# One scale for the a and b weights of a unit, with joint operations over both, and the last four pairs in the raw-query buffer: block-sparse attention followed by a bilinear FFN

## The chip, the cores and the metric

One core of one Trainium2 chip. The metric is the device time of one execution in microseconds (us); lower is better. The profile is one execution recorded by the hardware profiler, and all rows below are from it.

## The reference, cut to what matters

```python
# attention: batch 4, 8 heads, 768 positions, head size 64, blocks of 32
scores = q @ k.T / sqrt(64)
mask = (neighbour blocks) | (first and last block) | (3 sampled blocks per query block)
attn = softmax(where(mask, scores, -1e9))
attn_out = attn @ v
# FFN over the 3072 tokens, model size 512, inner size 1536
x = attn_out.transpose(0, 2, 1, 3).reshape(3072, 512)
out = ((x @ w_a) * (x @ w_b)) @ w_out
```

The inputs reach the kernel as 64-bit words of which it uses parts: the weights have to be put together from two 32-bit halves before they are numbers.

## The kernel before, in words

Every matrix product is made in fp16 with each operand split into a high part and a low part (hi and lo), after a scaling by a power of two that keeps them in range. TensorE multiplies hi by hi, hi by lo and lo by hi.

The attention runs in 96 units, one for a batch and a block of 32 queries. 88 of them are sparse (eight blocks of keys), eight are dense (the first and the last block of each batch). Eight units make a chunk of 256 tokens; there are 12 chunks, three for a batch. The FFN of a chunk can begin when the outputs of its eight units lie in xT, which is the event x_ready. The FFN runs over 12 inner blocks f of 128 columns. For each (chunk, f) there are 24 matmuls into ab (line 1265), then ScalarE and VectorE form a*b and split it (1282, 1285, 1294, 1297), and 6 matmuls add to the output (1325 to 1327). The first two chunks run f by f in three groups (0 to 5, 6 to 8, 9 to 11), so that they can begin before all the weights are ready.

The order of every engine's instructions is written out ahead by a planner (class Plan): each flow is a generator that yields an operation with an estimated duration or an event, and the planner always takes the operation that can begin first by its own estimates. The engines then execute their lists strictly in order. A changed estimate or a changed flow can thus alter the lists of all engines from that point on.

The weights are the flows weights(n) and weight_parts(n, ...), with n = 3f + i: i = 0 is w_a of block f, 1 is w_b, 2 is w_out. For each there are a load (752) into a raw ring of six slots, three VectorE operations that put the words together (768, 772, 775), a Square on ScalarE that sums into a bound (801), a scale for the three matrices of the block (weight_scale: a GpSimd reduction and four small VectorE operations, 826 to 837), a Copy to the high part on ScalarE (806) and a VectorE operation for the low part (809).

For f = 0 to 7 a and b are put together by joint operations over 1024 columns, into the place in wab that the weights of f + 4 will take later. From the Square on, a and b go separately, with 512 columns each. For f = 8 to 11 there is no such place: a and b are put together separately, in slots of the ring st, which has three slots and also serves w_out and the rows of the output. The three matrices of one block therefore fill that ring.

The buffer rq has one slot. queries(cc) takes it for the raw queries of a chunk and lets it go when the low part of the queries is made (708). The ring's takers are served in the order in which their flows ask for it.

All loads of raw keys and values of batches 1 to 3 wait for the event w_freed, which fires when the last weight has been put together (the raw weights lie in their buffers). The load of q is issued on ScalarE's queue (691), as are those of the weights and of raw keys (491).

Of the kernel before, what the change touches and what calls it, by code (L numbers as in the profile page):

```python
# [11 lines left out]
F32 = mybir.dt.float32  # L12
# [3 lines left out]
AF = mybir.ActivationFunctionType  # L16
# [21 lines left out]
AHEAD = 4  # L38
# [22 lines left out]
R_W, R_W_STEP = 16, 0.2  # L61
# [165 lines left out]
def dve(ns, fn):  # L227
    return [Way("DVE", ns, fn)]


def act(ns, fn):
    return [Way("ACT", ns, fn)]


def pool(ns, fn):
    return [Way("POOL", ns, fn)]


def load_way(moved, fn):

    return [Way("LOAD", 475, fn, moved)]
# [7 lines left out]
def kernel(  # L249
# [13 lines left out]
    nc = tc.nc  # L263
    B, NCH, D, H, CH = q.shape
    NF, P, DM = w_a.shape
# [5 lines left out]
    KT = DM // P  # L271
# [11 lines left out]
    work = ctx.enter_context(tc.tile_pool(name="work", bufs=2))  # L283
# [4 lines left out]
    plan = Plan()  # L288
    rings = {}

    def take(tag, bufs):
        return rings.setdefault(tag, Ring(bufs)).take()
# [5 lines left out]
    wab = wpool.tile([P, NF, 2, 2, KT, P], F16, name="wab")  # L298
# [15 lines left out]


    at_k, at_v, at_q, at_w = 0, B * NG, B * NG + B, B * NG + B + NC
    at_x = at_w + 3 * NF
    n_at = at_x + NC
    bound = const.tile([P, n_at], F32, name="bound")
    bound_v = const.tile([P, B * NG], F32, name="bound_v")  # L320
# [1 line left out]
    scale = const.tile([P, n_at], F32, name="scale")  # L322
    rscale = const.tile([P, n_at], F32, name="rscale")
# [45 lines left out]
    s_sent = {u: Event() for u in units}  # L369
    av_done = {u: Event() for u in units}  # L370
    x_ready = [Event(PER) for _ in range(NC)]
    w_bound = [Event(3) for _ in range(NF)]
    w_known = [Event(hi - lo) for lo, hi in GROUPS]
    all_known = Event(len(GROUPS))
    w_scale = [Event() for _ in range(NF)]
    w_staged = {}
    w_freed = Event(3 * NF)
    w_ready = [Event(3) for _ in range(NF)]
    w_small = [Event() for _ in range(NF)]
    ffn_done = [Event() for _ in range(NC)]  # L380

# [356 lines left out]
    def raw_weights(n, count):  # L738
        half, at = divmod(n % W_BUFS, W_BUFS // 2)
        raw = (  # L740
            stage.rearrange("p g x -> p (g x)"), keysT[1].rearrange("p h s -> p (h s)")
        )[half].bitcast(I32)
        return raw[:, at * 2 * DM : (at + count) * 2 * DM]

    def weights(n):

        f, i = divmod(n, 3)
        both = i == 0 and f + AHEAD < NF
        freed = []
        for m in range(n, n + 1 + both):  # L750
            freed.append((yield from take("w", W_BUFS)))
            yield load_way(1350, lambda m=m: nc.scalar.dma_start(
                raw_weights(m, 1), (w_a, w_b, w_out)[m % 3][f].bitcast(I32)
            ))
        if n + 1 + both < 3 * NF:
            plan.start(weights(n + 1 + both), R_W + R_W_STEP * (n + 1 + both))
        if both:

            if f + AHEAD >= NF // 2:
                yield parked  # L760
            w = wab[:, f + AHEAD].rearrange("p i a c x -> p (i a c x)").bitcast(F32)
            gone = w_staged[f + AHEAD, 0] = w_staged[f + AHEAD, 1] = Event(2)
        else:
            gone = yield from take("st", ST_BUFS)
            w = work.tile([P, DM], F32, tag="st", name=f"w{n}", bufs=ST_BUFS)
        words = raw_weights(n, 1 + both).rearrange("p (x w) -> p x w", w=2)
        o = w.bitcast(I32)
        yield dve(700 if both else 425, lambda: nc.vector.tensor_scalar(
            o, words[:, :, 1], 3, 0x3FFFFFFF, ALU.logical_shift_left, ALU.bitwise_and
        ))  # L770
        ns = 1220 if both else 685
        yield dve(ns, lambda: nc.vector.scalar_tensor_tensor(
            o, words[:, :, 0], 29, o, ALU.logical_shift_right, ALU.bitwise_or
        ))
        end = yield dve(ns, lambda: nc.vector.scalar_tensor_tensor(
            o, words[:, :, 1], -0x40000000, o, ALU.bitwise_and, ALU.bitwise_or
        ))
        for ev in freed:
            ev.fire(end)
            w_freed.fire(end)  # L780
        for m in range(1 + both):
            plan.start(
                weight_parts(n + m, w[:, m * DM : (m + 1) * DM], gone),
                R_W + R_W_STEP * (n + m), end,
            )

    def weight_parts(n, w, gone):
        f, i = divmod(n, 3)
        if i < 2:
            hi, lo = wab[:, f, i, 0], wab[:, f, i, 1]  # L790
            w = w.rearrange("p (c f) -> p c f", c=KT)
            if f >= NF // 2:
                yield parked
            if f >= AHEAD:
                yield w_staged[f, i]
        else:
            hi, lo = woh[:, f, :], wol[:, f, :]
            plan.start(weight_scale(f), R_W + R_W_STEP * n)
        at = at_w + 3 * f + i
        s = scale[:, at : at + 1]  # L800
        end = yield act(800, lambda: nc.scalar.activation(
            hi, w, AF.Square, accum_out=bound[:, at : at + 1]
        ))
        w_bound[f].fire(end)
        yield w_scale[f]
        end = yield act(720, lambda: nc.scalar.activation(hi, w, AF.Copy, scale=s))
        if i == 2:
            plan.start(small_weights(f, hi), R_W + R_W_STEP * n, end)
        end = yield dve(755, lambda: nc.vector.scalar_tensor_tensor(
            lo, w, s, hi, ALU.mult, ALU.subtract  # L810
        ))
        gone.fire(end)
        w_ready[f].fire(end)

    def small_weights(f, hi):
        end = yield act(620, lambda: nc.scalar.activation(
            wos[:, f, :], hi, AF.Copy, scale=1 / G_LOW
        ))
        w_small[f].fire(end)

    def weight_scale(f):

        yield w_bound[f]
        a = slice(at_w + 3 * f, at_w + 3 * f + 3)
        bits = power[:, a].bitcast(I32)
        yield pool(480, lambda: nc.gpsimd.partition_all_reduce(
            power[:, a], bound[:, a], P, bass_isa.ReduceOp.absmax
        ))
        yield dve(150, lambda: nc.vector.tensor_scalar(
            bits, bits, 1, 0x7F800000, ALU.logical_shift_right, ALU.bitwise_and  # L830
        ))
        yield dve(150, lambda: nc.vector.tensor_scalar(
            rscale[:, a], power[:, a], float(2.0 ** 53), float(2.0 ** -80), ALU.mult, ALU.max
        ))
        end = yield dve(160, lambda: nc.vector.reciprocal(scale[:, a], rscale[:, a]))
        w_scale[f].fire(end)
        end = yield dve(212, lambda: nc.vector.scalar_tensor_tensor(
            w3[:, f : f + 1], rscale[:, a.start : a.start + 1],
            rscale[:, a.start + 1 : a.start + 2], rscale[:, a.stop - 1 : a.stop],
            ALU.mult, ALU.mult,  # L840
        ))
        g = group_of(f)
        w_known[g].fire(end)
        if w_known[g].count == 0:
            lo, hi = GROUPS[g]
            end = yield dve(150, lambda: nc.vector.reduce_max(
                w3_max[:, g : g + 1], w3[:, lo:hi], axis=mybir.AxisListType.X
            ))
            group_known[g].fire(end)
            all_known.fire(end)  # L850
            if all_known.count == 0:
                n = len(GROUPS)
                end = yield dve(150, lambda: nc.vector.reduce_max(
                    w3_max[:, n : n + 1], w3_max[:, :n], axis=mybir.AxisListType.X
                ))
                group_known[n].fire(end)

    def group_of(f):
        return next(g for g, (lo, hi) in enumerate(GROUPS) if lo <= f < hi)
# [510 lines left out]
    with tc.manual_schedule():  # L1370
        nc.vector.memset(warm, 0.0)
        nc.vector.memset(bound, 0.0)
        nc.scalar.activation(warm, warm, AF.Exp)
        plan.start(keys(0, 0), -LEAD_K)
        plan.start(load_eye(), -LEAD_K)
        plan.start(queries(0), 0.5 - LEAD_K)
        plan.start(make_tables(), 0)
        plan.start(values(0, 0), -LEAD_V)
        plan.start(weights(0), R_W)
        plan.start(gather_keys(0), -LEAD_G)  # L1380
        plan.start(gather_values(0), -LEAD_G)
        plan.start(attend(*units[0]), 0)
        for cc in range(NC):
            plan.start(norms(cc), R_NOW)
        plan.start(first_products(), R_P1)
        plan.run()
# [69 lines left out]
```

## Time and profile before

| | us |
|---|---|
| median of 3 runs | 872.83 (871.74 to 878.28) |
| the profiled execution | 871.27 |
| span from its first to its last instruction | 869.5 |

So 1.8 us of the profiled execution lie outside its span, and the median stands 1.56 us above it. Busy times in the rows are those of one engine in a stretch; PE is TensorE, DVE is VectorE, ACT is ScalarE, POOL is GpSimd, and a q behind a name is that engine's queue of commands. A line Lnn is a line of the kernel before.

### The profile page before, as it was taken

How to read it: one execution, taken by the hardware profiler on the slowest of the kernel's cores; microseconds unless marked ns; L12 is line 12 of the kernel's file. 1: busy time of each engine (PE TensorE's matmuls, PEld its weight loads, DVE VectorE, ACT ScalarE, POOL GpSimd, SP SyncE). 2: the span in 40 equal slices, each digit the busy share in tenths (PEclk: the TensorE clock that was granted, in tenths of full speed). 3: DMA queues.
4: the chain of work that ended last, by engine and by line, in shares of the span. 5: the costliest groups of instructions: out<-in, count | busy, mean ns of one | idle time of the engine just before them, and what ended most of it. 6: DMA issues, size and time to landing. Idle time of an engine off the chain costs nothing.

```text
span 869.5 us, 24163 instructions
## 1 busy us (share of the span) xinstructions
PE 759.1 (87%) x9136; PEld 561.9 (65%) x9136; DVE 590.8 (68%) x1609; ACT 501.3 (58%) x1191; POOL 191.7 (22%) x428
## 2 busy tenths in 40 slices
PE   2246367599999979999999999999999999999998
PEld 1134245377767757766776667677777677777775
DVE  4979988999788666766576696766677776432222
ACT  6579787866766464774355586644656554332222
POOL 0743253200034232330032242200342310000000
PEclk9996689999999999999999999999999999999999
DMA  8766798795967479896586899767966766610000
GB/s 244 211 182 201 223 228 188 179 246 128 243 172 183 118 155 215 194 176 178 134 166 170 162 209 239 160 152 172 168 143 161 144 138 159 142 44 1 25 2 25
DMA packets 195151, 138.74 MB, mean 160 GB/s; under 512 B 138073, under 2 KB 162650, under 8 KB 195034
## 3 DMA queue, kind: packets, MB, share of 16 engines
q1 hardware_dynamic: 183104, 99.40, 52.3%
q10 hardware_dynamic: 11930, 37.79, 14.4%
q8 instruction: 72, 1.18, 0.6%
q14 instruction: 45, 0.37, 0.1%
HBM read 86.28 MB, written 12.58 MB: 114 GB/s over the span
## 4 chain that ended last, share of the span: by engine, by line
PE 47%; DVE 18%; DMA 18%; ACT 10%; issue 4%; SPq 2%; ACTq 1%; POOL 0%; POOLq 0%; DVEq 0%
PE ab L1265 25%; DMA pt<-hl 6%; PE av L967 5%; PE o L1325 5%; DMA q<-in_q_dram 5%; PE o L1327 4%; PE o L1326 4%; PE s L923 3%; DVE hl L948 2%; DMA VG<-vd 2%; DMA stage<-in_k_dram 2%; DVE QT L708 2%; DVE xT L1236 2%; ACT sm L1049 1%; ACT QT L706 1%
## 5 line engine op out<-in xcount | busy, mean ns | idle before, releaser
L1265 PE MATMUL ab<-xT,wab 128*128 128x256 f16 x3456 | 401.4, 273 | 6.0 <-DVE xT L1236 3.2
L1265 PEld LDWEIGHTS <-wab 128*128 128x128 f16 x3456 | 334.4, 98 | 68.5 <-issue 13.8
L1285 DVE SCALAR_TENSOR_TENSOR a<-a,to_g,ab 128x256 f32<-128x256 f32 x144 | 68.6, 477 | 104.8 <-ACT a L1282 103.7
L1282 ACT ACTIVATE a<-ab,w 128x256 f32<-128x256 f32 x144 | 67.3, 467 | 112.0 <-PE ab L1265 109.6
L1049 ACT ACTIVATE sm<-s,low,cq 128x256 f32<-128x256 f32 x176 | 97.7, 557 | 50.0 <-DVE low L1042 28.2
L948 DVE SCALAR_TENSOR_TENSOR hl<-sm,den,hl 128x256 f16<-128x256 f32 (+1 forms) x208 | 104.8, 512 | 27.7 <-ACT hl L941 25.5
L627 POOL COPY KG<-keysT 128x384 int32<-128x384 int32 x88 | 58.7, 667 | 283.5 <-PE s L923 251.4
L967 PEld LDWEIGHTS <-VG 128*128 128x128 f16 x2688 | 97.9, 100 | 29.3 <-issue 14.7
L1325 PE MATMUL o<-woh,gh 128*128 128x512 f16 x288 | 109.8, 381 | 7.9 <-ACT gh L1294 7.9
L967 PE MATMUL av<-pt,VG 128*128 128x64 f16 x2688 | 104.3, 196 | 11.0 <-DMA VG<-vd 7.4
L1327 PE MATMUL o<-wos,gl 128*128 128x512 f16 x288 | 109.3, 380 | 3.1 <-DVE gl L1297 2.6
L632 POOL COPY KG<-keysT 128x128 int32 x264 | 103.5, 428 | 36.7 <-POOL KG L627 26.3
L1326 PE MATMUL o<-wol,gh 128*128 128x512 f16 x288 | 109.2, 379 | 0.0
L1294 ACT ACTIVATE gh<-a 128x256 f16<-128x256 f32 x144 | 59.4, 413 | 60.6 <-DVE a L1285 55.8
L1297 DVE SCALAR_TENSOR_TENSOR gl<-gh,a 128x256 f16<-128x256 f16 x144 | 63.2, 440 | 34.2 <-ACT gh L1294 33.4
L941 ACT ACTIVATE hl<-sm,den 128x256 f16<-128x256 f32 (+1 forms) x91 | 46.0, 517 | 38.6 <-DMA pt<-hl 27.8
L923 PE MATMUL s<-KG,QT 128*32 128x256 f16 x1408 | 60.1, 295 | 6.6 <-POOL KG L632 6.1
L1236 DVE SCALAR_TENSOR_TENSOR xT<-av,xT 64x256 f16<-64x256 f32 x96 | 40.3, 420 | 33.0 <-ACT xT L1233 31.6
L1039 DVE TENSOR_REDUCE low<-s 128x2 f32<-128x512 f32 x88 | 60.0, 682 | 1.7 <-PE s L923 1.1
L1024 PE MATMUL s<-mrows,ident 128*32 128x192 bf16 (+1 forms) x352 | 25.9, 284 | 37.2 <-ACT sm L1049 25.3
L944 DVE TENSOR_SCALAR hl<-sm,den 128x256 f16<-128x256 f32 (+1 forms) x117 | 42.5, 365 | 19.7 <-DMA pt<-hl 19.4
L1327 PEld LDWEIGHTS <-gl 128*128 128x128 f16 x288 | 28.1, 98 | 42.4 <-DVE gl L1297 10.6
(115 smaller groups left out, 776.9 us busy)
## 6 DMA issues: line engine op xcount, KB each, us to landing
VG<-vd SPq DMA_DIRECT2D x284, 64.0 KB, 2.0
VG<-vd SPq DMA_DIRECT2D x88, 192.0 KB, 3.0
VG<-vd SPq DMA_DIRECT2D x32, 384.0 KB, 3.5
q<-in_q_dram ACTq DMA_DIRECT2D x24, 256.0 KB, 5.7
QT<-QT SPq DMA_DIRECT2D x24, 256.0 KB, 3.8
vd<-vs SPq DMA_DIRECT2D x16, 384.0 KB, 3.3
out_dram<-ou SPq DMA_DIRECT2D x24, 256.0 KB, 2.4
stage<-in_k_dram ACTq DMA_DIRECT2D x12, 384.0 KB, 5.5
```

Of the source, the lines that this page charges most:

```text
L632: nc.gpsimd.tensor_copy(to[:, :, (5 + r) * w : (6 + r) * w], of[:, :, bass.ds(at, w)])
L923: mm(to[h * BLK : (h + 1) * BLK], q_block(cc, i, 4 * hq + h, a), rhs(4 * hq + h), start=(first and a == 0), stop=(a == 1), skip_group_chec ...
L948: t = yield dve(221 + n * 1.03, lambda: nc.vector.scalar_tensor_tensor(lo, sm, over, hi, ALU.mult, ALU.subtract))
L967: mm(av[:, g, i % 2, :], w, pt[:, y, cols], start=(i % 2 == 0 and g == 0 and first and n + m == 0), stop=(last and n == len(terms) - 1 and ...
L1049: t = yield act(750, lambda hq=hq: nc.scalar.activation(sm[:, hq], ps[:, hq], AF.Exp, bias=low[:, at, hq, 0:1], scale=cq[:, cc, hq : hq + ...
L1265: mm(ab[:, i, :], wab[:, f, i, part, kt, :], xc[:, kt, a, :], start=(i == 0 and kt == 0 and part + a == 0), stop=(kt == KT - 1 and a == 1) ...
L1282: yield act(470, lambda: nc.scalar.activation(a_sb, ab[:, 0, :], AF.Copy, scale=w3[:, f : f + 1]))
L1285: t = yield dve(420, lambda: nc.vector.scalar_tensor_tensor(a_sb, a_sb, to_g[:, n : n + 1], ab[:, 1, :], ALU.mult, ALU.mult))
L1297: t = yield dve(460, lambda: nc.vector.scalar_tensor_tensor(gl, gh, -G_LOW, a_sb, ALU.mult, ALU.add))
L1325: mm(po, gh[:, js], woh[:, f, :], start=(f == lo), stop=False)
L1326: mm(po, gh[:, js], wol[:, f, :], start=False, stop=False)
L1327: mm(po, gl[:, js], wos[:, f, :], start=False, stop=(f == hi - 1))
```

## The change

The a and b weights of a block get one scale between them, from one bound over both; w_out keeps its own. The Square, the Copy to the high part and the low part are then made for both in one instruction over 2 x 512 columns, where there were two instructions over 512. The last four blocks also put a and b together by joint operations; their buffer is the one slot of rq in place of two slots of st. The planner's durations are altered to match. The product of the scales in weight_scale uses the shared scale twice.

```diff
-        both = i == 0 and f + AHEAD < NF
+        both = i == 0
...
-        if both:
+        if both and f + AHEAD >= NF:
+            gone = yield from take("rq", 1)
+            w = work.tile([P, H, CH], F32, tag="rq", name=f"w{n}", bufs=1)
+            w = w.rearrange("p h s -> p (h s)")[:, : 2 * DM]
+        elif both:
...
-            gone = w_staged[f + AHEAD, 0] = w_staged[f + AHEAD, 1] = Event(2)
+            gone = w_staged[f + AHEAD] = Event()
...
-        for m in range(1 + both):
-            plan.start(
-                weight_parts(n + m, w[:, m * DM : (m + 1) * DM], gone),
-                R_W + R_W_STEP * (n + m), end,
-            )
+        plan.start(weight_parts(n, w, gone), R_W + R_W_STEP * n, end)
...
-        if i < 2:
-            hi, lo = wab[:, f, i, 0], wab[:, f, i, 1]
-            w = w.rearrange("p (c f) -> p c f", c=KT)
+        if i == 0:
+            hi, lo = (
+                wab[:, f, :, a].rearrange("p i c f -> p i (c f)") for a in range(2)
+            )
+            w = w.rearrange("p (i x) -> p i x", i=2)
...
-        end = yield act(800, lambda: nc.scalar.activation(
+        end = yield act(1240 if i == 0 else 800, lambda: nc.scalar.activation(
             hi, w, AF.Square, accum_out=bound[:, at : at + 1]
         ))
...
-        end = yield act(720, lambda: nc.scalar.activation(hi, w, AF.Copy, scale=s))
+        end = yield act(1140 if i == 0 else 720, lambda: nc.scalar.activation(
+            hi, w, AF.Copy, scale=s
+        ))
...
-        end = yield dve(755, lambda: nc.vector.scalar_tensor_tensor(
+        end = yield dve(1290 if i == 0 else 755, lambda: nc.vector.scalar_tensor_tensor(
             lo, w, s, hi, ALU.mult, ALU.subtract
         ))
...
-        a = slice(at_w + 3 * f, at_w + 3 * f + 3)
+        a = slice(at_w + 2 * f, at_w + 2 * f + 2)
...
             w3[:, f : f + 1], rscale[:, a.start : a.start + 1],
-            rscale[:, a.start + 1 : a.start + 2], rscale[:, a.stop - 1 : a.stop],
+            rscale[:, a.start : a.start + 1], rscale[:, a.start + 1 : a.stop],
```

## Rows read from the trace of the kernel before

**Rows 1.** The page's first part: busy time, share of the span, instructions.

```profile
PE 759.1 (87%) x9136; PEld 561.9 (65%) x9136; DVE 590.8 (68%) x1609; ACT 501.3 (58%) x1191; POOL 191.7 (22%) x428
```

**Rows 2.** Stretches: length, busy PE, PEld, DVE, ACT, POOL (count), granted clock, DMA share, GB/s.

```profile
20.00:60.00 40.00, 10.87 (x134) 7.13 (x134) 33.95 (x79) 24.50 (x53) 21.90 (x34) 1.00 0.74 215
60.00:115.00 55.00, 30.08 (x482) 21.55 (x483) 52.75 (x128) 47.21 (x111) 21.43 (x36) 0.70 0.75 208
115.00:173.00 58.00, 39.49 (x548) 28.40 (x546) 51.15 (x143) 45.69 (x110) 19.74 (x37) 0.96 0.85 195
173.00:252.00 79.00, 78.53 (x830) 59.45 (x830) 68.12 (x185) 52.84 (x124) 7.31 (x21) 1.00 0.82 197
...
296.00:330.00 34.00, 29.59 (x418) 21.46 (x417) 24.53 (x71) 19.88 (x51) 9.19 (x22) 1.00 0.62 136
```

**Rows 3.** PE's timeline, first products of chunks 1 and 3: start, us, [idle before, releaser].

```profile
171.75 0.38 PE L1265 MATMUL ab<-xT,wab 128*128 128x256 f16 x2 [0.85 <-ACT xT L1233]
173.14 2.56 PE L1265 MATMUL ab<-xT,wab 128*128 128x256 f16 x22 [1.01 <-DVE xT L1236]
...
326.06 2.56 PE L1265 MATMUL ab<-xT,wab 128*128 128x256 f16 x22 [0.67 <-DVE xT L1236]
```

**Rows 4.** Groups by line and form, whole span: busy us, mean ns of one.

```profile
L708 DVE SCALAR_TENSOR_TENSOR QT<-q,scale,QT 64x2048 f16<-64x2048 f32 x12 | 28.2, 2347 | 5.8 <-ACT QT L706 5.7
L706 ACT ACTIVATE QT<-q,scale 64x2048 f16<-64x2048 f32 x12 | 24.0, 2000 | 2.4 <-DVE scale L399 2.2
L809 DVE SCALAR_TENSOR_TENSOR wab<-wab,scale 128x512 f16<-128x512 f32 x16 | 12.1, 760 | 0.0
L806 ACT ACTIVATE wab<-wab,scale 128x512 f16<-128x512 f32 x16 | 10.8, 711 | 0.5 <-DVE scale L835 0.4
L801 ACT ACTIVATE wab<-wab 128x512 f16<-128x512 f32 x16 | 9.9, 622 | 6.2 <-DVE wab L775 5.9 <-DVE den L1054 0.2
L772 DVE SCALAR_TENSOR_TENSOR w<-stage,w 128x512 int32<-128x512 int32 x10 | 6.8, 676 | 0.0
L809 DVE SCALAR_TENSOR_TENSOR wab<-w,scale,wab 128x512 f16<-128x512 f32 x8 | 5.8, 747 | 0.4 <-ACT wab L806 0.4
L772 DVE SCALAR_TENSOR_TENSOR wab<-stage,wab 128x1024 int32<-128x1024 int32 x4 | 4.9, 1237 | 0.0
L801 ACT ACTIVATION_READ_ACCUMULATOR wab<-wab 128x1 f32 x16 | 3.0, 189 | 0.0
```

**Rows 5.** Waits from 20 to 173 us: waiter, awaited, us in total, times, longest.

```profile
DVE hl L948 <- ACT hl L941: 10.5, 4, 4.6
...
PE s L1024 <- ACT sm L1049: 22.7, 9, 4.6
```

**Rows 6.** DVE's timeline: words of f = 8 to 11, and the queries of chunk 3.

```profile
146.72 0.76 DVE L768 TENSOR_SCALAR w<-stage 128x512 int32<-128x512 int32 x2
162.95 0.42 DVE L768 TENSOR_SCALAR w<-stage 128x512 int32<-128x512 int32 x1
169.90 2.34 DVE L708 SCALAR_TENSOR_TENSOR QT<-q,scale,QT 64x2048 f16<-64x2048 f32 x1 [0.47 <-ACT QT L706]
176.50 0.41 DVE L768 TENSOR_SCALAR w<-keysT 128x512 int32<-128x512 int32 x1
192.40 0.42 DVE L768 TENSOR_SCALAR w<-stage 128x512 int32<-128x512 int32 x1
...
214.39 0.69 DVE L775 SCALAR_TENSOR_TENSOR w<-keysT,w 128x512 int32<-128x512 int32 x1
```

**Rows 7.** ScalarE's timeline: loads of block 8's b, chunk 3's queries, batch 1's first keys.

```profile
136.30 0.33 ACTq L752 DMA_DIRECT2D stage<-in_moe_w_b_dram  x1
...
157.50 0.61 ACTq L691 DMA_DIRECT2D q<-in_q_dram  x1
...
215.12 0.96 ACTq L491 DMA_DIRECT2D stage<-in_k_dram  x2
```

**Rows 8.** PE's timeline: the first scores of batch 1 (unit 24).

```profile
237.06 0.83 PE L923 MATMUL s<-keysT,QT 128*32 128x384 f16 x16
```

More of the change, by code (lines that the diff above doesn't have):

```diff
@@ L316 @@
     at_k, at_v, at_q, at_w = 0, B * NG, B * NG + B, B * NG + B + NC
-    at_x = at_w + 3 * NF
+    at_x = at_w + 2 * NF
     n_at = at_x + NC
@@ L371 @@
     x_ready = [Event(PER) for _ in range(NC)]
-    w_bound = [Event(3) for _ in range(NF)]
+    w_bound = [Event(2) for _ in range(NF)]
     w_known = [Event(hi - lo) for lo, hi in GROUPS]
@@ L377 @@
     w_freed = Event(3 * NF)
-    w_ready = [Event(3) for _ in range(NF)]
+    w_ready = [Event(2) for _ in range(NF)]
     w_small = [Event() for _ in range(NF)]
@@ L794, in weight_parts @@
             if f >= AHEAD:
-                yield w_staged[f, i]
+                yield w_staged[f]
         else:
@@ L798, in weight_parts @@
             plan.start(weight_scale(f), R_W + R_W_STEP * n)
-        at = at_w + 3 * f + i
+        at = at_w + 2 * f + (i > 0)
         s = scale[:, at : at + 1]
-        end = yield act(800, lambda: nc.scalar.activation(
+        end = yield act(1240 if i == 0 else 800, lambda: nc.scalar.activation(
             hi, w, AF.Square, accum_out=bound[:, at : at + 1]
```

## The prediction

> **What bounds the kernel now.** I read the page's first part, then busy time by stretch, then the timeline of TensorE where the stretches change, then the waits of the early stretch.
>
> The first part [rows 1] names TensorE, with 87% of the span. That is an average over two different halves, and the table of stretches [rows 2] separates them. From 173 to 252 us TensorE is busy 78.53 of 79 us. From there on it nearly always has an FFN product to do, and what is taken from VectorE or ScalarE buys nothing. Before 173 us it is busy less than 70% of the time, with part of that at a granted clock of 0.70. There VectorE is the full engine: 33.95 of 40, 52.75 of 55 and 51.15 of 58 us, so 137.85 of 153 from 20 to 173 us. ScalarE stands beside it with 117.4 of 153.
>
> The change of regime has one cause [rows 3]: the FFN of chunk 1 starts at 171.75 us, stops after two matmuls and goes on at 173.14, waiting both times for xT, the attention output of that chunk. So the end is the moment when chunk 1's eight units are done, plus TensorE's remaining work, plus its later idle time. A second such place is the first product of chunk 3 at 326.06 us, again with a wait for xT [rows 3]; the 34 us around it hold 4.4 us of TensorE idle time [rows 2], the densest after 173 us. Chunk 3 is the first of batch 1, and batch 1 can only begin when the last weight has been put together: 214.39 plus 0.69 us on VectorE [rows 6], the first raw keys issued at 215.12 [rows 7], the first scores at 237.06 [rows 8].
>
> The change touches both places: it takes work from VectorE and ScalarE before 173 us, and it alters the queue of buffers that ends at 215 us.
>
> **Work removed.** Durations are from [rows 4].
> - Low part on VectorE: 24 instructions of 512 columns (16 of 760 ns, 8 of 747) become 12 of 1024. No row has that shape. Between 512 columns (747) and 2048 (2347, the queries' low part, the same operation on 64 partitions) the slope is 1.042 ns a column, so 1024 come to 1280 ns. 17.9 us become 15.4.
> - Words of f = 8 to 11: three operations for a and three for b become three. The one that is shown costs 2 x 676 = 1352 against 1237 ns, 115 saved; the other two have the same pattern. 4 x 3 x 115 ns = 1.4 us.
> - Square on ScalarE: 622 ns and a read of the accumulator of 189, twice per block. I take the slope of the Copy, (2000 - 711) / 1536 = 0.839 ns a column, so 1024 come to 1052 ns. A block saves 2 x 622 - 1052 = 192, and one read of 189: 381 ns.
> - Copy on ScalarE: 2 x 711 = 1422 against 711 + 430 = 1141 ns, 281 saved.
>
> In all VectorE loses 2.5 + 1.4 = 3.9 us and ScalarE 12 x 0.66 = 7.9 us. The scale's small operations keep their count and lose one column each, which I price at nothing.
>
> What the Trainium skill says of this (Perfetto Trace Analysis, Optimizing Scalar/DVE Operations) is an access overhead of some 60 ns for an instruction on VectorE and some 93 ns on ScalarE that grouping saves. By those figures the 24 instructions gone from VectorE would save 1.4 us and the 24 gone from ScalarE 2.2, an estimate well below the rows' 3.9 and 7.9; the pair of 676 and 1237 ns in this trace [rows 4] decides for the larger figure.
>
> **What of it lies on the path before 173 us.** Blocks 0 to 7 are finished by then, and the Squares and words of block 8 [rows 6]. On VectorE that is 12.1 - 8 x 1.28 = 1.9 us of low parts and 0.35 us of words: 2.2 us. On ScalarE it is 9 x 0.381 + 8 x 0.281 = 5.7 us. What this is worth is between two bounds. At least nothing: VectorE has 15 idle us from 20 to 173, 10.5 of them waiting for ScalarE's high part of the attention weights [rows 5], and TensorE's largest wait there, 22.7 us, is for the exponentials [rows 5], which a planner's order and not an engine's load may set. At most both sums, 7.9 us, if the two engines form one chain throughout. VectorE is 90% busy, so I take most of its 2.2 us, and of ScalarE's 5.7 us, on an engine at 77%, about a fifth: together **3.0 us**. If the attention chain is what sets 173 us, and not the load, this term is zero.
>
> A cost stands against it. A joint Copy and low part take 1.14 + 1.28 = 2.42 us in series, where Copy b ran beside the low part of a: 0.71 + 2 x 0.76 = 2.23. That is 0.2 us later for a block; the weights are needed in order and the first products of chunk 0 do not wait for anything of them that would be seen, so it is hidden while xT comes last. A joint instruction also keeps an attention operation behind it waiting up to 0.53 us longer (1280 - 747 ns); that is inside the four fifths of ScalarE's share that I leave out.
>
> The skill has a rule that speaks against the joint forms (the same section): where these engines are not saturated but make bubbles on others, smaller instructions can let work finish sooner. TensorE's 22.7 us of waits for the exponentials before 173 us [rows 5] are such bubbles. The rival "nothing gained" below is what the rule would give here.
>
> **The queue for rq.** Before, a, b and w_out of block 9 had to wait for the three slots of st that block 8 held. The first word operations of blocks 8, 9 and 10 stand at 146.72, 176.50 and 192.40 us [rows 6]; the 15.9 us between blocks 9 and 10 is the time for which a block holds its slots. Block 8 stretched to 30 us because its w_out waited for a slot until 162.95 [rows 6].
>
> After, w_out alone uses st, so that wait goes. But a and b share one slot with the raw queries. Block 8 asks for it when its b load is issued, at 136.30 us [rows 7]. The queries of chunk 3 ask only when unit 19 has its scores, and their load went out at 157.50 [rows 7]. So I expect the order block 8, queries 3, block 9, 10, 11. Queries 3 hold the slot from 157.50 [rows 7] to 169.90 + 2.34 [rows 6], 15 us, most of it the transfer. Their load stands on ScalarE's queue and now waits there for block 8's low part; behind it are the exponentials. By the planner's order it is issued when the slot is due, so I price this wait at nothing; were the plan 1 us early, it would cost about that once. Nobody needs queries 3 before 237 us [rows 8], so their delay is hidden by some 60 us.
>
> The last words are then together at 146.7 + three holds + 15 + 5 us (the words of block 11). Against 215.1 us the balance lies at 48.4 us for three holds, **16 us each**. A hold's own work is three word operations (at most 1.24 each), Square with its read 1.24, Copy 1.14 and low part 1.28, so 7.4 us alone on its engines, and the scale's small operations. The hold before, 15.9 us, was longer by six 512-column word operations in place of three joint ones and by w_out's words, which had to wait for a slot in the same ring. I take 12 to 13 us, between the two. Then the last words are ready near 205 us, 10 us sooner, and batch 1 begins so much sooner. TensorE has no free time until 252, so only the idle 4.4 us around the start of chunk 3 [rows 2] can shrink. I take a third: **1.5 us**. The bounds are a gain of 4.4 and, with holds of 20 us, a loss of 12 (last words at 227), since the start of chunk 3 has no slack.
>
> **The sum.** 871.27 - 3.0 - 1.5 = 866.8 us for a profiled execution; the median stands 1.56 above it, so **868.3 us**.
>
> **The rivals.**
> - Nothing gained. The chain through exponentials, high parts and transposes sets 173 us, not the load, or the planner's new order gives the 3 us back in other small waits. For it: the 10.5 and 22.7 us of waits [rows 5], and that every list after the first weight is written anew. Against: VectorE at 52.75 of 55 us. Time: 872.8, by 2 either way.
> - Both engines count in full, and batch 1's earlier start fills the idle time: 872.8 - 7.9 - 4.4 = 860.5 us. For it: VectorE waits for ScalarE where it waits at all. Against: 77% is not a full engine.
> - Slower: the single slot of rq strings out the last weights. Holds of 20 us put the last words at 227, batch 1 and the start of chunk 3 12 us later, with TensorE idle for it: 872.8 - 3 + 12 = 881.8 us. It decides from 16 us a hold. For it: the hold before was 15.9 us, and a slot too few now joins five takers one behind the other. Against: the words start with a buffer that is really free, and w_out is out of the queue.
> - The change does less than it says: a joint instruction could cost twice a single one, since its output lies in two pieces. The joint word operations show no such thing (1237 against 676), so I give it nothing of its own; it would end as "nothing gained".
>
> **How the numbers follow.** My forecast has 0.46, nothing gained 0.22, both in full 0.19, slower 0.13. A measurement of this kernel tells about 1% from no change, so the bounds are 864.1 and 881.6 us. Faster by over 1%: the second rival and a little of the forecast, 0.22. Slower by over 1%: 0.11, as that rival's smaller prices remain inside. Within 1%: 0.67. The range goes from 860, where the second rival stands, to 879, which leaves out the worst of the third; most of its width comes from the two unknown bounds, the share of ScalarE's 5.7 us and the length of a hold.
>
> **What would show it.** The first FFN product of chunk 1 at 169 to 171 us where it was 171.75; joint low parts near 1280 ns and joint Copies near 1140 ns; the load of queries 3 after block 8's low part; the first raw keys of batch 1 near 205 us and the first scores near 227; the stretch from 173 us on as full as before. The prediction is wrong if chunk 1 starts at the same time although VectorE has less to do, if the raw keys come after 215 us, or if TensorE's idle time after 252 us differs by more than some 5 us from the lists being written anew.

## The result, and the profile after

| | before | after |
|---|---|---|
| median of 4 runs, us | 873.11 (871.74 to 878.28) | 882.14 (880.49 to 885.29) |
| the profiled execution, us | 871.27 | 882.27 |
| its span, us | 869.5 | 880.3 |

The ratio is 1.0106 with an interval of 1.007 to 1.0142: slower by 9 us, where 4.5 us of gain were forecast. Ratios, here and below, leave out executions over 1.5% above the fastest of their kernel, at most two of an altered kernel's but four of the ten of e4b below, which average 0.9985 of before with these and have the ratio 0.9933 without. The page's first part beside [rows 1]: TensorE has the same 9136 matmuls and is busy 9.7 us longer, at a granted clock of 0.961 over the span where it was 0.978. VectorE and ScalarE have lost 2.3 and 5.0 us.

```profile
PE 768.8 (87%) x9136; PEld 567.0 (64%) x9136; DVE 588.5 (67%) x1587; ACT 496.3 (56%) x1153; POOL 190.6 (22%) x428
```

The stretches of [rows 2] in the changed kernel:

```profile
20.00:60.00 40.00, 10.63 (x130) 6.20 (x131) 33.75 (x75) 24.25 (x49) 23.02 (x36) 1.00 0.73 210
60.00:115.00 55.00, 28.80 (x430) 20.92 (x434) 52.13 (x126) 44.19 (x94) 16.79 (x30) 0.64 0.74 221
115.00:173.00 58.00, 45.11 (x604) 32.89 (x604) 54.42 (x146) 41.56 (x101) 19.95 (x41) 0.84 0.90 204
173.00:252.00 79.00, 73.56 (x753) 54.92 (x753) 56.12 (x146) 49.80 (x107) 5.48 (x15) 0.96 0.84 168
...
296.00:330.00 34.00, 31.63 (x420) 23.46 (x412) 20.65 (x55) 17.15 (x42) 7.33 (x18) 1.00 0.66 141
```

Count the matmuls. From 20 to 173 us both kernels made 1164. From 173 to 252 us, where TensorE was full before, the changed kernel makes 753 where there were 830. At 79 / 830 = 0.095 us each, these 77 are 7.3 us. Idle time and clock come to about the same: TensorE is busy 5.0 us less, and a granted clock of 0.96 in place of 1.00 is 3.2 us of 79. So in these two traces most of the loss is there by 252 us, and not where the gain was expected. From 252 to 750 us TensorE is as busy as before and the lost work isn't made up (the kernel before, then the changed one):

```profile
252.00:750.00 498.00, 479.98 (x6159) 355.62 (x6159) 346.15 (x983) 288.74 (x715) 118.98 (x291) 1.00 0.75 168
```
```profile
252.00:750.00 498.00, 479.68 (x6119) 353.86 (x6118) 347.91 (x988) 289.45 (x713) 123.08 (x299) 1.00 0.76 167
```

The first products of chunks 1 and 3, for [rows 3], say the same: chunk 1 is no earlier (173.30 and 174.28 for 171.75 and 173.14), chunk 3 is 8 us late (334.15 for 326.06).

```profile
173.30 0.38 PE L1269 MATMUL ab<-xT,wab 128*128 128x256 f16 x2 [2.46 <-ACT xT L1237]
174.28 4.23 PE L1269 MATMUL ab<-xT,wab 128*128 128x256 f16 x22 [0.61 <-DVE xT L1240]
...
334.15 2.56 PE L1269 MATMUL ab<-xT,wab 128*128 128x256 f16 x22 [0.67 <-DVE xT L1240]
```

The same 22 products take 4.23 us where they took 2.56 [rows 3]. That is not the change's doing alone: in e6 below, which is no slower than the kernel before, they take 4.67.

Groups by line and form, for [rows 4]; L813 is the low part, L808 the Copy, L803 the Square, L776 the words:

```profile
L813 DVE SCALAR_TENSOR_TENSOR wab<-wab,scale 128x1024 f16<-128x1024 f32 x8 | 10.2, 1274 | 0.0
L808 ACT ACTIVATE wab<-wab,scale 128x1024 f16<-128x1024 f32 x8 | 9.2, 1144 | 0.1
L803 ACT ACTIVATE wab<-wab 128x1024 f16<-128x1024 f32 x8 | 8.4, 1052 | 8.1 <-DVE wab L779 8.1
L776 DVE SCALAR_TENSOR_TENSOR w<-stage,w 128x1024 int32<-128x1024 int32 x2 | 2.4, 1216 | 0.0
```

Waits from 20 to 173 us, for [rows 5]. Those two are shorter, and chunk 1 is no earlier for it; TensorE's wait for the high part of the attention weights (the second row) has grown from 7.6 us, the last row, which is of the kernel before:

```profile
PE s L1028 <- ACT sm L1053: 15.1, 4, 4.6
...
PE pt_t L1105 <- ACT hl L945: 12.1, 5, 7.0
...
DVE hl L952 <- ACT hl L945: 7.1, 3, 4.8
```
```profile
PE pt_t L1101 <- ACT hl L941: 7.6, 3, 5.2
```

VectorE's timeline, for [rows 6]: first words operation (L772) and joint low part (L813) of the pairs of blocks 8, 9, 10, 11, and the low part of chunk 3's queries (L708).

```profile
140.32 0.69 DVE L772 TENSOR_SCALAR w<-stage 128x1024 int32<-128x1024 int32 x1
...
164.95 1.28 DVE L813 SCALAR_TENSOR_TENSOR wab<-w,scale,wab 128x1024 f16<-128x1024 f32 x1
...
167.87 0.68 DVE L772 TENSOR_SCALAR w<-keysT 128x1024 int32<-128x1024 int32 x1
...
177.53 1.28 DVE L813 SCALAR_TENSOR_TENSOR wab<-w,scale,wab 128x1024 f16<-128x1024 f32 x1
...
193.99 2.35 DVE L708 SCALAR_TENSOR_TENSOR QT<-q,scale,QT 64x2048 f16<-64x2048 f32 x1 [1.29 <-ACT QT L706]
196.65 0.68 DVE L772 TENSOR_SCALAR w<-stage 128x1024 int32<-128x1024 int32 x1
...
214.09 0.69 DVE L772 TENSOR_SCALAR w<-keysT 128x1024 int32<-128x1024 int32 x1
216.80 1.22 DVE L779 SCALAR_TENSOR_TENSOR w<-keysT,w 128x1024 int32<-128x1024 int32 x1
```

The slot's order is block 8, block 9, queries 3, block 10, block 11. The last pair's words end at 216.80 + 1.22 = 218.02 us. ScalarE's timeline, for [rows 7], shows the load of chunk 3's queries 25 us later than before (157.50) and batch 1's first keys 3 us later (215.12):

```profile
182.42 0.61 ACTq L691 DMA_DIRECT2D q<-in_q_dram  x1
...
218.06 0.82 ACTq L491 DMA_DIRECT2D stage<-in_k_dram  x2
```

The first scores of batch 1, for [rows 8], are 9 us late (237.06 before):

```profile
245.85 0.83 PE L927 MATMUL s<-keysT,QT 128*32 128x384 f16 x16
```

Of the 79 - 73.56 = 5.4 us in which TensorE stands idle there, most lies in two holes, at 197 and 230 us. Its timeline shows what ended them, and the waits of ScalarE from 173 to 252 us show who was late: its list stands 4.7 us at raw keys and 4.2 us at the high part of attention weights, whose buffer hl a transposing DMA is still reading.

```profile
198.52 0.88 PE L971 MATMUL av<-pt,VG 128*128 128x64 f16 x24 [1.80 <-DMA pt<-hl]
...
230.41 0.69 PE L971 MATMUL av<-pt,VG 128*128 128x64 f16 x18 [1.54 <-DMA pt<-hl]
231.71 0.39 PE L1329 MATMUL o<-woh,gh 128*128 128x512 f16 x1 [0.62 <-ACT gh L1298]
```
```profile
ACT ks L501 <- DMA stage<-in_k_dram: 4.7, 3, 3.6
ACT hl L945 <- DMA pt<-hl: 4.2, 1, 4.2
```

From 220 to 240 us, in the kernel before and then in the changed one (columns as in [rows 2]), TensorE goes from full to 17.27 of 20 us, the granted clock falls, and the matmuls from 196 to 145:

```profile
220.00:240.00 20.00, 20.00 (x196) 15.11 (x195) 15.81 (x47) 13.17 (x27) 1.51 (x4) 1.00 0.97 229
```
```profile
220.00:240.00 20.00, 17.27 (x145) 12.20 (x144) 12.13 (x38) 11.71 (x22) 1.51 (x4) 0.91 0.84 167
```

### The profile page after: what moved, and what is told of

Read it like the earlier page. It is cut to its first block, busy times and chain, and to the rows that moved or that the text cites. A ratio compares the mean times of both kernels' runs of the same rounds, so it can differ in the third digit from the quotient of the medians.

```text
span 880.3 us, 24100 instructions
## 1 busy us (share of the span) xinstructions
PE 768.8 (87%) x9136; PEld 567.0 (64%) x9136; DVE 588.5 (67%) x1587; ACT 496.3 (56%) x1153; POOL 190.6 (22%) x428
## 4 chain that ended last, share of the span: by engine, by line
PE 44%; DMA 9%; DVE 8%; ACT 6%; issue 3%; SPq 2%; ACTq 0%; POOLq 0%; POOL 0%; DVEq 0%
PE ab L1269 24%; PE av L971 4%; PE o L1329 4%; PE o L1331 4%; PE o L1330 4%; DMA q<-in_q_dram 3%; PE s L927 2%; DMA pt<-hl 2%; DMA keysT<-ks 1%; DVE hl L952 1%; DMA VG<-vd 1%; ACT sm L1053 1%; DVE QT L708 1%; ACT QT L706 1%; DVE a L1289 1%
## 5 line engine op out<-in xcount | busy, mean ns | idle before, releaser
L971 PEld LDWEIGHTS <-VG 128*128 128x128 f16 x2688 | 101.3, 102 | 31.0 <-issue 16.0
L971 PE MATMUL av<-pt,VG 128*128 128x64 f16 x2688 | 107.6, 199 | 13.2 <-DMA VG<-vd 6.6
L1237 ACT ACTIVATE xT<-av 64x256 f16<-64x256 f32 x96 | 36.0, 375 | 34.6 <-PE av L971 33.8
```

Source lines behind the costliest of these rows:

```text
L971: mm(av[:, g, i % 2, :], w, pt[:, y, cols], start=(i % 2 == 0 and g == 0 and first and n + m == 0), stop=(last and n == len(terms) - 1 and ...
```

## The experiments

Single executions of the kernel before took from 866 to 884 us, so ratios to it with their intervals decide; a trace is one execution and tells where its time lies. The theories: (1) joint work is worth nothing or holds up attention; (2) the ring rq strings out the last weights, the third rival; (3) the new lists are bad by chance; (4) the last four pairs' move out of ring st costs, by some part of it. In the overview, q is the start of the first of the two commands that load chunk 3's queries (the rows show the second), and PE and mm are the busy time and the matmuls of TensorE from 173 to 252 us; a dash stands where none is given.

| kernel | ratio (95%) | q | PE | mm |
|---|---|---|---|---|
| before | 1 | 156.98 | 78.53 | 830 |
| e4_replan | 1.0029 (0.9992 to 1.0067) | 160.58 | 75.12 | 777 |
| e4b_replan_up | 0.9933 (0.9896 to 0.9971) | - | - | - |
| f3_before_keys | 0.9939 (0.9897 to 0.9982) | 155.37 | 79.00 | 792 |
| e6_same_lists | 0.9998 (0.9966 to 1.003) | 155.12 | 78.39 | 810 |
| e12_up_joint | 0.9993 (0.9958 to 1.0027) | 154.69 | 78.55 | 820 |
| e2_first8 | 1.0023 (0.9981 to 1.0064) | 167.27 | 71.95 | 767 |
| after | 1.0106 (1.007 to 1.0142) | 181.88 | 73.56 | 753 |
| e5_after_replan | 1.0102 (1.0047 to 1.0158) | - | - | - |
| e5b_after_replan_up | 1.0151 (1.0098 to 1.0203) | 210.79 | 76.03 | 826 |
| e8_keys_slow | 1.0047 (1.0013 to 1.0081) | 179.40 | 75.24 | 798 |
| e9_q3_last | 1.017 (1.0114 to 1.0226) | 208.61 | 73.89 | 786 |
| f1_st_tokens | 1.0124 (1.0002 to 1.0245) | 180.49 | 75.05 | 786 |
| e1_place | 1.0162 (1.0084 to 1.024) | 164.28 | 72.56 | 774 |
| f4_place_keys | 1.0042 (1.0007 to 1.0076) | 159.22 | 75.91 | 808 |
| e3_words_rq | 1.0084 (1.0045 to 1.0122) | 170.11 | 74.12 | 769 |
| e11_words_q3_last | 1.0051 (1.001 to 1.0092) | 217.33 | 73.57 | 771 |
| g1_single_rq | 1.0107 (1.0048 to 1.0167) | 189.72 | 75.71 | 796 |
| g2_q3_late | 1.0143 (1.0091 to 1.0194) | 184.62 | 75.20 | 734 |

**Is joint work worth anything?** e2 has the joint operations and the one scale in blocks 0 to 7 only; blocks 8 to 11 are as before. e6 goes further and keeps the planner's flows and durations of before: of each pair's two operations in blocks 0 to 7 the first is left out of the list, and the joint one stands at the place of the second.

```diff
-        end = yield act(720, lambda: nc.scalar.activation(hi, w, AF.Copy, scale=s))
+        end = yield act(720, lambda: second("copy", lambda: nc.scalar.activation(
+            hi, w, AF.Copy, scale=s
+        )))
```

> One scale and joint Square, Copy and low part for blocks 0 to 7 alone; blocks 8 to 11 as in the kernel before, with st and three scales. Theory ring: the queue for rq is not touched, 868 to 873 us. Theory joint: chunk 1 is no earlier and the loss is there, 878 to 882. Theory lists: anywhere from 868 to 884.

> The lists of the kernel before, instruction by instruction, but for blocks 0 to 7 the first of each two (Square a, Copy a, low part a) is left out and the second is the joint instruction over both, with one scale. The planner sees the kernel before. So it has the joint work without new lists. Theory lists (the loss is in the new order, the joint work itself is harmless): no slower than before, 868 to 875 us, chunk 1 at 173 us or up to 3 us sooner. Theory joint (long instructions hold up the attention): 878 us or more, chunk 1 later than 174.

Measured: 1.0023 and 0.9998. With lists otherwise those of before, the work that the change takes away in blocks 0 to 7 buys nothing that shows; e6's interval, 0.9966 to 1.003, reaches from 3.0 us of gain to 2.6 us of loss. e6's first products of chunk 1 stand where they were, though VectorE and ScalarE have less to do:

```profile
172.02 0.58 PE L1284 MATMUL ab<-xT,wab 128*128 128x256 f16 x2 [0.86 <-ACT xT L1252]
173.41 4.67 PE L1284 MATMUL ab<-xT,wab 128*128 128x256 f16 x22 [0.81 <-DVE xT L1255]
```

Theory 1 falls on its second half too: the joint instructions do no harm there.

e2 shows one thing more. From 173 to 252 us it makes hardly more matmuls than the changed kernel (767 to 753), and in the end it is not slower: from 252 to 750 us TensorE is busy 8 us longer than before.

```profile
252.00:750.00 498.00, 487.99 (x6266) 363.08 (x6265) 351.92 (x989) 290.73 (x721) 116.56 (x291) 1.00 0.74 170
```

So a poor stretch up to 252 us need not be a loss: later idle time can take it up. Why e2 can and the changed kernel can't isn't shown.

**Is it a chance of the lists?** The planner's durations of the weights' operations are altered by 10 ns, which reorders all later lists and changes no instruction: e4 down and e4b up in the kernel before, e5 and e5b in the changed one, e12 up in e6.

```diff
-        end = yield act(800, lambda: nc.scalar.activation(
+        end = yield act(790, lambda: nc.scalar.activation(
```

> The kernel before, the same instructions, but the planner is told durations 10 ns shorter for the weights' Square, Copy and low part (790, 710, 745), so that all lists after the first weight may come out in another order. It measures how much the order alone moves the time. Theories ring and joint: 872 to 875 us, nothing else has changed. Theory lists: 5 us or more away from 873, on either side.

> The kernel before, the same instructions, the planner told durations 10 ns longer for the weights' Square, Copy and low part. Theory lists: a third value for the same work, 3 us or more from the kernel before, more likely slower, since the lists of the kernel before were kept by choice. Theory that order alone costs little: within 3 us of before.

> The changed kernel, the same instructions, the planner told durations 10 ns shorter for the weights' Square, Copy and low part. Theory lists: the time moves by 4 us or more from 882, more likely downward. Theory that the changed buffers themselves cost 9 us: 880 to 884 us.

> The changed kernel, the same instructions, planner durations 10 ns longer for the weights' Square, Copy and low part. Theory ring: again 1.008 to 1.012 of before, third group stalled by 4 us or more behind the second. Theory lists: 3 us or more off that, on either side.

> The kernel before with planner durations 10 ns longer (0.9933 of before), and in its lists, for blocks 0 to 7, the joint Square, Copy and low part at the second one's place. If the joint work is harmless and worth little: 0.990 to 0.996 of before. If it holds up the attention: 0.998 or more. Nothing of blocks 8 to 11 is joined.

Measured: the lists alone move the kernel before from 0.9933 to 1.0029. The changed kernel stays at 1.0102 and 1.0151. Taken pair by pair, at equal nudges, the change costs 1.0106, 1.0102 / 1.0029 = 1.0073, and 1.0151 / 0.9933 = 1.0219. So a chance of half a per cent is likely, and it isn't the cause. e12 (0.9993) missed its expectation for harmless joint work, 0.990 to 0.996, and against e4b it is 0.6% slower; as e4b's ratio is so uncertain (0.9985 with all of its executions), this shows no gain from joint work, and whether joint work costs something in that order stays open.

**Is it the queue for rq?** e1_place takes three of the four pairs out of the queue: they are put together in the wab places of blocks 9, 10 and 11, which are still free. e9 leaves the pairs in rq and lets the queries of chunk 3 ask after all of them.

```diff
+        if both and NF - AHEAD <= f < NF - 1:
+            held = w_staged[f + 1]
+            gone = w_staged[f + 1] = Event()
+            yield held
+            w = wab[:, f + 1].rearrange("p i a c x -> p (i a c x)").bitcast(F32)
```
```diff
+        if cc == 3:
+            yield last_pair
         freed = yield from take("rq", 1)
```

> The changed kernel, but the words of pairs 8, 9 and 10 are put together in the places of wab that belong to blocks 9, 10 and 11 (free once the pair four blocks earlier is done), and only pair 11 uses the slot of rq; so queries 3 no longer stand in one queue with the last weights. Theory ring (the single slot of rq delays the last weights and with them batch 1): the 9 us go, 870 to 874 us, keys of batch 1 issued before 212 us. Theory lists (all lists are written anew, and the new ones lose by small waits at other places): anywhere from 872 to 884, without relation to when the keys go out. Theory joint (long instructions hold up the attention): 880 to 883.

> The changed kernel, with the queries of chunk 3 asking for the slot of rq only after all four pairs have had it; nothing up to their old place in that queue is altered. Theory ring (block 10 and 11 wait for queries 3, so the third group of chunk 0's FFN stalls): words of block 10 near 182 us where they were 196.65, the keys of batch 1 near 205, first product of the third group within 4 us of the second group's last, 872 to 877 us. Theory lists (the order alone): no relation, 876 to 886 us.

Measured: the last words come early, and batch 1's first keys of e1_place leave at 204.56 us, as I had forecast for the change itself. It is no faster than the changed kernel all the same, 1.0162, and e9 is at 1.017; both are slower than any of the theories had said. Theory 2 falls twice. The two rows are of e1_place: the load, and the stretch from 173 to 252 us.

```profile
204.56 0.34 ACTq L491 DMA_DIRECT2D stage<-in_k_dram  x1
```
```profile
173.00:252.00 79.00, 72.56 (x774) 53.95 (x773) 65.01 (x170) 56.93 (x126) 8.38 (x21) 0.95 0.86 201
```

**ScalarE's wait for the keys.** The list ran into keys that had not landed, so in e8 the planner counts 2500 ns in place of 1000 for each load of batch 1's raw keys. f3 does the same to the kernel before and f4 to e1_place.

```diff
-        yield load_way(1000, lambda: nc.scalar.dma_start(raw, k[b, g]))
+        yield load_way(2500 if b == 1 else 1000, lambda: nc.scalar.dma_start(raw, k[b, g]))
```

> The changed kernel, but the planner is told 2500 ns in place of 1000 for each load of batch 1's raw keys, so that ScalarE's list takes up these keys later; nothing before 215 us is altered. If the 5 us that the changed kernel loses between 226 and 237 us come from ScalarE waiting in its list for these keys: first product of the third group (chunk 0, f = 9) at 232 us or sooner where it was 236.6, and 876 to 879 us in all. If that stall is only the place where an earlier loss shows: 881 to 884 us.

> The kernel before, in which the planner counts 2500 ns in place of 1000 for each load of batch 1's raw keys. In the changed kernel this gave back 0.6%. If that was a repair of a fault of the change, it does nothing here: 0.997 to 1.003. If it is a better order for any of these kernels, 0.990 to 0.996, and the loss of the change stays at 1%.

> The kernel with the words of pairs 8 to 10 in the places of later blocks (1.0162), with the planner counting 2500 ns for each load of batch 1's raw keys. Theory 'lists into the keys': the loss falls by more than half, to 1.000 to 1.007. Theory 'pace' and theory 'words in other buffers': little change, 1.011 to 1.018.

Measured: e8 gains 0.6% on the changed kernel, which looked like a repair until the control: f3 gains 0.6% on the kernel before. The distance stays, 1.0047 / 0.9939 = 1.0109. f4 gains more on e1_place, and is still 1.0042 / 0.9939 = 1.0104 above f3.

**Which part of the last four pairs' move?** e3 is the kernel before in which only the words of pairs 8 to 11 are made jointly, in rq; Square, scales, Copy and low part are as before. e11 adds e9's edit to it. f1 is the changed kernel in which each of these pairs also holds two places of st, unused, so that st paces the last weights as it did.

```diff
+        if both and f + AHEAD >= NF:
+            e = yield from take("rq", 1)
+            w = work.tile([P, H, CH], F32, tag="rq", name=f"w{n}", bufs=1)
+            w = w.rearrange("p h s -> p (h s)")[:, : 2 * DM]
+            gone = Both(e)
```
```diff
+        if both and f + AHEAD >= NF:
+            s1 = yield from take("st", ST_BUFS)
+            s2 = yield from take("st", ST_BUFS)
+            gone = Many(gone, s1, s2)
```

> The kernel before, with only the words of pairs 8 to 11 joined in the slot of rq; three scales and separate Squares, Copies and low parts throughout. Theory ring: 879 to 884 us, the keys of batch 1 after 215 us. Theory joint: as before, 871 to 875. Theory lists: anywhere from 868 to 884; lists up to the words of block 8 nearly as before, so chunk 1 at 173 us.

> The kernel before with only the words of pairs 8 to 11 joined in the slot of rq (as in the run of words alone, 1.0084 of before), and the queries of chunk 3 behind all four pairs. Theory ring: 0.998 to 1.003 of before. Theory lists: 1.004 or more, as without the shift.

> The changed kernel, in which a pair of blocks 8 to 11 also has to hold two of the three places of the ring st (which it does not write to) until its low part is made, as in the kernel before. Theory 'pace': ring st held the last weights back and that suited the attention; with the pace back the ratio to the kernel before falls from 1.0106 to 1.00, 0.997 to 1.004. Theory 'lists into the keys': the pace is not the point, the ratio stays at 1.008 to 1.013. Theory 'chance of the order': anything from 0.995 to 1.013.

Measured: e3 1.0084, with nothing of the scale or of the joint Square, Copy and low part in it. e11 is at 1.0051. f1 is at 1.0124: the fall to 1.00 that the pace theory wanted isn't seen, though the wide interval just reaches it. f2, which gives e1_place the same two places to hold, ended after 241.51 us with 1828 of the 9136 matmuls made, so the same pace without the queue for rq stays untried.

The last two take e3 apart. g1 makes a and b one by one, as before, in the two halves of the slot of rq. g2 is the kernel before with a single change: the queries of chunk 3 wait for the words of block 9's b.

```diff
+        if i < 2 and f + AHEAD >= NF:
...
+            t, gone = pair_tile[f]
+            w = t[:, i * DM : (i + 1) * DM]
```
```diff
+        if cc == 3:
+            yield words9
         freed = yield from take("rq", 1)
...
+        if n == 28:
+            words9.fire(end)
```

> The kernel before, in which a and b of blocks 8 to 11 are put together one by one as before, but in the two halves of the slot of rq. The same words made jointly gave 1.0084. Theory 'the joint form of the last words costs': 0.996 to 1.003 here. Theory 'leaving st costs, by the other buffer and the queue in it': 1.005 to 1.012, and TensorE busy under 76.1 us from 173 to 252 us, as in the ten kernels of that kind.

> The kernel before with one change: the queries of chunk 3 ask for their buffer only when the words of block 9's b are made, so that their load goes out near 178 us in place of 157, as in the changed kernel. The buffers of the weights are as before. Theory 'the moved queries cost': 1.005 to 1.012. Theory 'they are hidden', as the prediction priced them: 0.996 to 1.004, and TensorE busy 77 to 79 us from 173 to 252 us.

Measured: g1 1.0107, so the joint form is not the cost. g2 1.0143: with every weight's buffer and instruction as before, later queries and the lists that come of them cost as much as the whole change. g2 was run in one order only, but it is 1.1% above the slowest order of the kernel before (1.0029). The rows of g2: ScalarE's timeline with the load at 185.14 us (157.50 before), the stretches, and TensorE's hole at 235 us, which waits for the same thing as in the changed kernel.

```profile
185.14 0.61 ACTq L694 DMA_DIRECT2D q<-in_q_dram  x1
```
```profile
173.00:252.00 79.00, 75.20 (x734) 56.00 (x734) 62.77 (x169) 49.72 (x110) 6.35 (x18) 0.95 0.83 185
220.00:240.00 20.00, 16.66 (x133) 12.42 (x132) 16.39 (x51) 13.34 (x29) 1.55 (x4) 0.91 0.90 163
```
```profile
235.65 1.02 PE L972 MATMUL av<-pt,VG 128*128 128x64 f16 x18 [2.71 <-DMA pt<-hl]
```

From 220 to 240 us g2 has 133 matmuls, the changed kernel 145, the kernel before 196.

## Why the prediction was wrong, point by point

The sum held two gains, 3.0 and 1.5 us, and neither came. On top of that came a loss for which the sum has no term.

- **What bounds the kernel.** Right that TensorE is full from 173 us on in the kernel before, and that chunk 1's xT opens that regime. Wrong to conclude that little can be lost there: in the two traces the full stretch held most of the loss. Wrong also to count a microsecond at chunk 1 as one at the end. The rows are of e12, where chunk 1 begins 6.5 us sooner than before (171.75) and the span is 869.0 us for 869.5, and of e2, where it begins 6.8 us later and the span is 870.9:

```profile
165.29 0.38 PE L1284 MATMUL ab<-xT,wab 128*128 128x256 f16 x2 [0.89 <-ACT xT L1252]
```
```profile
178.58 0.59 PE L1271 MATMUL ab<-xT,wab 128*128 128x256 f16 x2 [2.56 <-ACT xT L1239]
```

- **The sizes of the removed work** were right as durations: 1274 to 1282 ns for the joint low part (1280 forecast), 1138 to 1144 for the Copy (1141), 1052 to 1057 for the Square (1052), 1216 for a word operation (1237). Of the totals, 2.3 and 5.0 us are gone where 3.9 and 7.9 were summed. The new lists also made two copies of transposed attention weights (pt) on VectorE (1.4 us) that ScalarE had made (2.0 us), so the change itself took away some 3.7 and 3.0 us. ScalarE's share is small because neighbouring instructions overlap: in the kernel before the durations of its groups add up to 577.6 us, and it is busy for 501.3. The overheads that the Trainium skill gives (Perfetto Trace Analysis, Optimizing Scalar/DVE Operations) are busy times, of which the profiled latency is about twice as much, as the section says; the prediction set them against durations. Here ScalarE's 3.0 us are nearer to the 2.2 of that estimate, and VectorE's 3.7 us to the rows' 3.9.
- **What the work is worth: 3.0 us forecast, none seen** (e6 0.9998, e2 1.0023). The failing step is "VectorE is 90% busy, so I take most of its 2.2 us". The prediction named the condition itself, "if the attention chain is what sets 173 us, and not the load, this term is zero". In e6's trace, with the list order kept, chunk 1 goes on at 173.41 us for 173.14. Less work on nearly full engines didn't move it, so there the load didn't set it. The Trainium skill's rule in that section, that breaking up instructions may let work finish sooner where engines that aren't saturated make bubbles on others, isn't borne out either: joining did no harm in e6.
- **The queue: 1.5 us of gain, measured a loss.** The order was wrong in one place: the queries came after block 9 and not after block 8. Block 8 held the slot from 140.32 to 164.95 + 1.28 us, 26 us where 12 to 13 were taken: the scale waits for the bound of w_out too, and the Square of block 8's w_out came only at 156.19 us on ScalarE, 8 us after its words (147.23 + 0.68), a wait that the sum for a hold leaves out; blocks 9 and 10 held it 11 and 15 us (167.87 to 178.81, 196.65 to 209.95 + 1.28), near the forecast. Nor was the queries' hold mostly the transfer: before, their load landed in 5.0 of the 15 us. Batch 1's keys left 3 us late, not 10 early. But even ten early wasn't worth a gain: e1_place had keys at 204.56 us and 1.0162.

```profile
156.19 0.62 ACT L803 ACTIVATE woh<-w 128x512 f16<-128x512 f32 x1
```

- **The step that took a price for nothing** is "nobody needs queries 3 before 237 us, so their delay is hidden by some 60 us". Their first use was far off, their work was not free: an ACTIVATE of 1.9 us and one of 2.0 on ScalarE, 2.35 us on VectorE, a load and two transfers on SP's queue came out of the time before 173 us, in which TensorE has idle time, into the stretch in which both engines must feed TensorE, in lists whose order can't give way. g2 makes that one delay and costs 1.43%, 12 us, where the sum had 0. It shows that the step is wrong in the kernel before; how much of the 9 us it is in the changed kernel isn't shown.
- **The third rival** had the right side and nearly the right time, 881.8 us for 882.14, by luck, as its mechanism didn't take place: the last weights were strung out by 3 us, not 12, and undoing the queue didn't help.
- **The list order** was named as an unknown. It moves the kernel before from 0.9933 to 1.0029.

**What stays open.** That late queries, with the lists that come of them, are enough to lose 1.4% in the kernel before is shown, in one order. That the 2.0 and 2.35 us pieces on the two feeding engines are what costs is argued, from where the holes lie; it isn't their load, as VectorE and ScalarE are less busy from 173 to 252 us than before (56.12 for 68.12 us, 49.80 for 52.84). The cause of the changed kernel's own loss stays open, since runs without the delay lose as much: f4 has them near their old time (159.22) and is 1% above its own control f3; e1_place has them 7 us late and loses 1.6%; e2 has them 10 us late, has a poor stretch from 173 to 252 us (71.95), and loses nothing in the end; e11 has them latest, 47 us later than e3, and loses no more than e3 (1.0051 for 1.0084). Nor does the stretch from 173 to 252 us decide: e5b makes 826 matmuls there and loses 1.5%. Leaving st with four pairs costs 0.4 to 1.7% in every form that was tried, and the part of that which comes without late queries isn't explained.

## What to carry to other kernels

When a change lends a buffer to another user, cost the old user's whole work at its new time, with its compute instructions and its transfers on every queue, and not only the distance to its first reader. Before you credit work taken from a 90% busy engine, keep the order and take only the work away: if the awaited event does not move, the load was not what set it. Then check that the end follows that event: here chunk 1 moved by 6 to 7 us either way and the end by less than 2 us. Where a planner writes the lists, nudge its estimates first to see what a new order alone does, and run every repair on the kernel before as a control; here the two lowest ratios (0.9933 and 0.9939) are the kernel before with other estimates.

## What the hardware showed that was not expected

The transposing DMAs of the attention weights took a median of 8.1 us to land among the four issued from 173 to 200 us in the changed kernel, where the queries' load and their two copies now run, against 5.0 before (the view of DMA issues of the kernel before, then of the changed one):

```profile
pt<-hl SPq DMA_TRANSPOSE x4, 5.0
```
```profile
pt<-hl SPq DMA_TRANSPOSE x4, 8.1
```

In g2 the same median is 5.1, so slow transposes go with the loss in one kernel and not in the other. The other surprise is what a short hole costs beyond itself: in both kernels with a hole between 220 and 240 us the granted clock of these 20 us reads 0.91 where it was 1.00, on top of 2.7 and 3.3 us without work. The rows show it: in the changed kernel this product takes 0.63 us behind the hole and 0.38 before and after it.

```profile
222.30 0.38 PE L1330 MATMUL o<-wol,gh 128*128 128x512 f16 x1
...
232.83 0.63 PE L1330 MATMUL o<-wol,gh 128*128 128x512 f16 x1
...
239.44 0.38 PE L1330 MATMUL o<-wol,gh 128*128 128x512 f16 x1
```

The missing 51 matmuls are a quarter of the 196, though TensorE was still busy 86% of the time. The hole of 2.7 us and the clock, 0.09 of 20 us or 1.8 us, are 23% of the stretch, so nearly all of it is hole and clock; little is left for another mix of matmuls.
